# Moving the block sums of a fused attention and feed-forward kernel from GpSimd to VectorE, with earlier operand splits and loads

## The chip, the cores and the metric

The kernel runs on one core of one Trainium2 chip. The metric is the device time of one execution in microseconds: before the change 1176.31 us (median of 3 runs, 1173.57 to 1179.24). The engines of the core work side by side, each through its own queue in the order in which the program issued: TensorE (PE) multiplies matrices, VectorE (DVE) and ScalarE (ACT) work element by element, GpSimd (POOL) does too and also issues DMAs, and SyncE (SP) only issues DMAs. PSUM, where PE writes, is used here in 8 banks.

## What is computed

The inputs are q, k and v of 8 batches, 12 heads, 448 positions and 64 channels, and two weight matrices in float64, w_in (768 x 2048) and w_out (2048 x 768).

```
scores = scale * np.matmul(q, k.transpose(0, 1, 3, 2)) - np.log(S)
attn = 1.0 / (1.0 + np.exp(-scores))
x = attn @ v                      # laid out as 3584 tokens x 768
h = x @ w_in
g = 0.5 * h * (1.0 + erf(h / sqrt(2)))
out = g @ w_out
```

So it is an attention with a sigmoid in place of softmax, and behind it a GELU feed-forward layer over 3584 tokens.

## The kernel before

**Attention** comes first: 24 units (a batch and two pairs of heads each), whose results are written to DRAM (`scr_x`). PE is busy throughout. Beside it DVE and ACT *decode* the weights: a float64 arrives as two 32-bit words and is turned into a float32 with five DVE and two ACT instructions a chunk (class `Decoder`, L97 to L192). There are 40 chunks: 16 of w_in (768 wide, each written to `scr_f`) and 24 of w_out (512 wide). `dec.to(n)` sets at which places of the program the work up to chunk n is issued.

**The feed-forward layer** runs over 4 blocks of 896 tokens (two batches). Each product is made exact enough by splitting both operands in a high and a low half (ACT casts to `hi`, DVE computes `lo = src - hi`) and adding three matmuls, `hi*lo + lo*hi + hi*hi` (`terms`, L467). Block 0 computes its first product (x times w_in) plainly, `ffn1_plain`: 16 rows of w_in, 36 matmuls each. All other products use a Strassen-Winograd scheme: 2 x 2 blocks, seven products (p = 1 to 7) in place of eight, and sums of blocks as operands. `ffn1` (first product, blocks 1 to 3) runs 56 steps of 9 matmuls in the order `IN_ORDER`: the chains (1, 2), (6, 7, 4) and (5, 3). `ffn2` (second product, all blocks) runs 28 steps of 18 matmuls in the order `OUT_ORDER`: p = 1, 2, 5, 6, 3, 7, 4 with four column groups c each. So the feed-forward part is seven stages of 504 matmuls behind one of 576.

Who prepares what:

- **Weights** (class `Weights`, L197): SP loads a unit into `wst` (3 places), ACT casts it (L233) and DVE subtracts (L234) into `whl` (4 places). A unit serves one step of `ffn2` or two of `ffn1`. `prepare_to` runs 3 to 4 units ahead of PE, and `load_to` another 2 to 3.
- **Sums of weight blocks** (`mix`, L88): four sums on POOL, for 6 groups of w_out (`flush`, in `ffn1_plain`, as soon as four chunks are decoded) and for 8 groups of w_in (`remix`, in `ffn2` of block 0). POOL issues the DMAs that write the sums to `scr_out` and `scr_in`, whence SP loads units.
- **Operands of `ffn2`** (`build`, L609): ACT casts a tile of `g` (L262) and DVE subtracts (L263) into `op`, two steps before PE uses it. Before the first step `build(0)` and `build(1)` are issued together.
- **Sums of operands**: `difference_g` (L501, in the first product), L672, L674 and L675 (in `ffn2`, in place in the tiles of g) and `x_sum` (L553), all on POOL. `x_split` (L558) splits the x operands of the next block; `x_load` fetches their four tiles with 12 DMAs on SP's queue.
- **Results** leave PSUM through ACT (L648, L650, L655, L585) or a sum on DVE (L589, L591, L595, L652, L660, L664).

The order on every engine is that of the program text; nothing is moved by a scheduler.

## Time and profile before

| | us |
|---|---|
| median of 3 runs | 1176.31 (1173.57 to 1179.24) |
| profiled execution | 1176.96 |
| its span, first to last instruction | 1175.2 |
| PE busy | 1071.8 (91%) |
| DVE busy | 838.6 (71%) |
| ACT busy | 607.3 (52%) |
| POOL busy | 400.8 (34%) |
| mean granted PE clock | 0.961 |

Times in the profile count from the first instruction. The stages begin, by the first matmul of each, at 0 (attention), 256.1 (`ffn1_plain`), 385.9 (`ffn2` of block 0), 517.6 (`ffn1` of block 1), 628.8 (`ffn2`), 740.9 (`ffn1` of block 2), 844.8 (`ffn2`), 959.4 (`ffn1` of block 3) and 1063.3 (`ffn2`). A row such as `L234 DVE TENSOR_TENSOR whl<-wst,whl` names the line of the kernel, the engine, the operation, and the tile written and those read. In square brackets, or behind the last bar, stands the idle time of the engine before the instruction and what ended it. "PE busy" counts a matmul as long as it is in the pipeline, so a busy PE may still be slow; what counts is how soon each step of 18 matmuls follows the other.

### The profile page before, as it was taken

Reading aid. Unit: us, or ns where it says so; the run is one execution under the profiler, and the core shown is the slowest. Engines: PE = TensorE matmul, PEld = TensorE weight load, DVE = VectorE, ACT = ScalarE, POOL = GpSimd, SP = SyncE. Lnnn points to the kernel's source line nnn. Section 1 sums busy time; section 2 is a strip of 40 time slices with the busy share of each in tenths; the row PEclk is TensorE's granted clock in tenths of the full one; section 3 lists DMA queues with packets and bytes.
Section 4 is the critical chain, followed back from the end, with each engine's and each line's share of the span. In section 5 each row is a group of like instructions: output and inputs, shape, how many; then the busy total and the mean of one; then the engine's idle time right before and its main releaser. Section 6 shows DMA issues by size and latency. Waiting matters only on the chain. (4 is left out here: it accounts for less than half of the span.)

```text
span 1175.2 us, 15595 instructions
## 1 busy us (share of the span) xinstructions
PE 1071.8 (91%) x5930; PEld 924.2 (79%) x5930; DVE 838.6 (71%) x852; ACT 607.3 (52%) x810; POOL 400.8 (34%) x316
## 2 busy tenths in 40 slices
PE   9999999999986876789997979999798999998988
PEld 4455455559986876679997969999797899987988
DVE  4777777648895579985566799556659974665895
ACT  5887887764343533236354624544454354445532
POOL 0111111037878479972011482000219310011640
PEclk9999999999998888889999989999899899998999
DMA  9999998775764695574332625433353443332332
GB/s 283 305 307 300 306 294 271 218 240 183 251 211 142 217 347 180 205 249 157 118 108 85 221 67 168 145 108 108 94 189 104 130 155 114 116 96 92 118 108 98
DMA packets 96378, 211.80 MB, mean 180 GB/s; under 512 B 10288, under 2 KB 47536, under 8 KB 96304
## 3 DMA queue, kind: packets, MB, share of 16 engines
q1 hardware_dynamic: 84560, 171.24, 46.8%
q0 software_dynamic: 11584, 39.33, 8.8%
q8 instruction: 47, 0.77, 0.3%
q10 hardware_dynamic: 160, 0.23, 0.1%
q14 instruction: 27, 0.22, 0.1%
HBM read 160.43 MB, written 50.33 MB: 179 GB/s over the span
## 5 line engine op out<-in xcount | busy, mean ns | idle before, releaser
L472 PE MATMUL pf<-op,whl 128*128 128x448 f32 x2016 | 415.2, 369 | 76.8 <-DVE op L263 49.5
L472 PEld LDWEIGHTS pf<-op,whl 128*128 128x128 f32 x2016 | 398.0, 199 | 94.0 <-DVE op L263 57.8
L234 DVE TENSOR_TENSOR whl<-wst,whl 128x768 fp32r<-128x768 f32 x212 | 282.1, 1332 | 182.0 <-ACT whl L233 181.8
L233 ACT CAST whl<-wst 128x768 fp32r<-128x768 f32 x212 | 175.9, 830 | 278.8 <-PE pf L472 198.7
L472 PE MATMUL pf<-xh_p,whl 128*128 128x448 f32 x1008 | 277.7, 355 | 11.8 <-DVE tmp L595 7.3
L472 PEld LDWEIGHTS pf<-xh_p,whl 128*128 128x128 f32 x1008 | 192.1, 191 | 15.4 <-issue 6.3
L263 DVE TENSOR_TENSOR op<-g,op 128x896 fp32r<-128x896 f32 x112 | 184.5, 1651 | 4.7 <-ACT op L262 4.7
L472 PE MATMUL pf<-xl_p,whl 128*128 128x448 f32 x504 | 179.1, 355 | 4.0 <-DVE xl_p L263 4.0
L328 ACT ACTIVATE a<-sc 128x896 f32<-128x896 f32 x144 | 121.8, 920 | 53.4 <-PE sc L345 53.4
L501 POOL TENSOR_TENSOR g<-g,g 128x896 f32<-128x896 f32 x16 | 34.3, 2145 | 299.2 <-ACT g L498 299.2
L383 PE MATMUL pav<-a,v 128*64 128x448 f32 x576 | 119.1, 548 | 0.0
L472 PE MATMUL pf<-xh,whl 128*128 128x448 f32 x384 | 106.0, 357 | 4.5 <-DVE whl L234 3.5
L262 ACT CAST op<-g 128x896 fp32r<-128x896 f32 x112 | 104.2, 935 | 4.7 <-POOL g L672 2.4
L472 PEld LDWEIGHTS pf<-xl_p,whl 128*128 128x128 f32 x504 | 96.1, 191 | 4.6 <-DVE xl_p L263 4.4
L498 ACT ACTIVATE g<-tmp 128x448 f32<-128x448 f32 x72 | 42.6, 621 | 98.4 <-DVE tmp L595 98.4
L383 PEld LDWEIGHTS pav<-a,v 128*64 128x64 f32 x576 | 37.0, 136 | 68.0 <-issue 63.6
L412 POOL DMA_DIRECT2D scr_x<-x x24 | 17.3, 719 | 208.7 <-DVE x L409 208.7
L472 PEld LDWEIGHTS pf<-xh,whl 128*128 128x128 f32 x384 | 73.5, 191 | 6.2 <-DVE whl L234 4.2
L409 DVE COPY x<-pav 128x448 f32<-128x448 f32 x48 | 29.9, 624 | 63.7 <-PE pav L383 40.9
L472 PE MATMUL pf<-xl,whl 128*128 128x448 f32 x192 | 68.6, 357 | 0.5 <-DVE xl L263 0.5
L672 POOL TENSOR_TENSOR g<-g,g 128x896 f32<-128x896 f32 x16 | 34.1, 2137 | 97.1 <-DVE op L263 97.0
L129 ACT ACTIVATE me<-me 128x512 f32<-128x512 int32 (+1 forms) x40 | 29.1, 728 | 55.1 <-DVE me L118 55.1
(70 smaller groups left out, 1213.1 us busy)
## 6 DMA issues: line engine op xcount, KB each, us to landing
wst<-scr_out SPq DMA_DIRECT2D x112, 384.0 KB, 3.1
wst<-scr_in SPq DMA_DIRECT2D x84, 384.0 KB, 3.0
v<-v_dram SPq DMA_DIRECT2D x24, 512.0 KB, 5.5
raw<-w_in_dram SPq DMA_DIRECT2D x16, 768.0 KB, 8.3
raw<-w_out_dram SPq DMA_DIRECT2D x24, 512.0 KB, 5.5
scr_x<-x POOLq DMA_DIRECT2D x24, 448.0 KB, 6.8
...
```

The costliest lines, as they stand in the source:

```text
L129: nc.scalar.activation(e.bitcast(F32), e.bitcast(I32), AF.Relu, bias=1151.0 * 2**23, scale=-8.0)
L233: nc.scalar.copy(hl[:, 0], t)
L234: nc.vector.tensor_tensor(hl[:, 1], t, hl[:, 0], op=ALU.subtract)
L262: nc.scalar.copy(hi, src)
L263: nc.vector.tensor_tensor(lo, src, hi, op=ALU.subtract)
L328: nc.scalar.activation(to, sc, AF.Sigmoid, bias=NEG_LOG_S, scale=SCALE)
L383: nc.tensor.matmul(pav[rows(j)], vals[u][:, p, j, c], a[:, j], start=p == 0 and c == 0, stop=p == 1 and c == FULL - 1,)
L409: nc.vector.tensor_copy(xs[u][:, p], bank(u, p))
L472: nc.tensor.matmul(bank, a, braid(m), **flags)
L498: nc.scalar.activation(straight(dst), unbraid(src), AF.Gelu)
L501: nc.gpsimd.tensor_tensor(g[0, 1][c], g[0, 1][c], g[0, 0][c], op=sub)
L672: nc.gpsimd.tensor_tensor(t1, g22, t1, op=sub)
```

## The change

- All sums that POOL computed (`mix`, `difference_g`, `x_sum` and the three sums in `ffn2`) are issued on DVE. POOL keeps its DMAs alone. The sum for p = 4 (L675) moves from the steps of p = 6 to those of p = 3.
- `scr_out` has one tensor for both halves of a column group, so a group is written with 7 DMAs instead of 14.
- `build` becomes a function of its own. The first two operands of an `ffn2` are split ahead: in block 0 in the last two rows of `ffn1_plain`, in the other blocks at (5, 3) and (5, 7) of `ffn1`.
- In attention 24 chunks are decoded instead of 22: 16 at the rate of before, one a unit, and 8 in the last six units. There the `hi` cast of p = 0 goes from ACT to DVE. `ffn1_plain` decodes the other 16 over 13 rows.
- `x_load` is issued at step 0 of `ffn2` instead of step 6, the first two `x_sum`s at step 7 instead of step 16. `x_split` of 6, 7, 5 and 3 stands at other places of `ffn1`; the `hi` half of x operand 7 gets a place of its own (the tag `s`), a fourth beside the three of `raw`.
- The sums of w_in come in two stages: groups 0 to 3 at steps 2, 8, 14 and 20 of `ffn2` of block 0, where `recopy` also copies the unmixed parts of groups 4 to 7 from DRAM to DRAM; and groups 4 to 7 in the first steps of `ffn1` of block 1, in tiles of g that are not yet in use.

```diff
     def mix(a, s):
-        a11, a12, a21, a22 = (a[:, i] for i in range(4))
-        s1, s2, s3, s4 = (s[:, i] for i in range(4))
-        nc.gpsimd.tensor_tensor(s1, a21, a22, op=ALU.add)
...
+        a11, a12, a21, a22 = a
+        s1, s2, s3, s4 = s
+        nc.vector.tensor_tensor(s1, a21, a22, op=ALU.add)
...
                 for p in (1, 2, 5, 6, 3, 7, 4):
                     src = parts[p].rearrange("p (h f n) -> p h f n", h=2, f=2)
-                    for h in range(2):
-                        nc.gpsimd.dma_start(scr_out[p, 2 * c + h][:, :, e], src[:, h])
+                    nc.gpsimd.dma_start(scr_out[p, c][:, :, :, e], src)
...
-    AHEAD, BEGIN = 22, 2
+    AHEAD, BEGIN, LATE = 24, 2, 18
...
-            if p == 0 and u > 2:
+            if p == 0 and 2 < u <= LATE:
                 nc.scalar.copy(hi, raw)
             else:
                 nc.vector.tensor_copy(hi, raw)
...
-                dec.to(min((u + 0.5 - BEGIN) * AHEAD / (total - BEGIN), AHEAD))
+                work = u + 0.5 - BEGIN
+                if work > NF:
+                    work = NF + (work - NF) * (AHEAD - NF) / (total - LATE)
+                dec.to(min(work, AHEAD))
...
         def difference_g(g, c):
-            nc.gpsimd.tensor_tensor(g[0, 1][c], g[0, 1][c], g[0, 0][c], op=sub)
+            nc.vector.tensor_tensor(g[0, 1][c], g[0, 1][c], g[0, 0][c], op=sub)
...
-                dec.to(AHEAD + 1.5 * (f + 1))
+                dec.to(AHEAD + (len(CHUNKS) + 0.5 - AHEAD) * (f + 1) / (NF - 3))
+                if f >= NF - 2:
+                    build(0, g, f - NF + 2)
...
         def x_sum(tag, b, p, a, c):
             t = x_tile(tag, f"x{b}_p{p}") if tag else c
-            nc.gpsimd.tensor_tensor(
+            nc.vector.tensor_tensor(
...
         def x_split(ops, b, p):
-            hi = ring(f"xh{b}_p{p}")
+            hi = ring(f"xh{b}_p{p}", "s" if p == 7 else "raw")
...
-                if (p, j) == (1, 2):
-                    x_split(ops, b, 6)
-                after = {(1, KF - 1): 7, (2, KF - 1): 4, (6, KF - 1): 5, (7, KF - 1): 3}
+                if b == 1 and p == 1 and KF // 2 <= j + 3 < KF:
+                    remix(j + 3, g)
+                after = {(1, 4): 6, (1, 6): 7, (2, KF - 1): 4, (7, 2): 5, (6, KF - 1): 3}
                 if (p, j) in after:
                     x_split(ops, b, after[p, j])
+                if (p, j) == (5, 3):
+                    build(b, g, 0)
+                if (p, j) == (5, KF - 1):
+                    build(b, g, 1)
...
-            build(0)
-            build(1)
             for n, (p, c) in enumerate(OUT_ORDER):
                 hl = W.get()
-                build(n + 2)
+                build(b, g, n + 2)
...
                 if ahead[0] == 5:
                     t1, g22 = g[0, 1][ahead[1]], g[1, 1][ahead[1]]
-                    nc.gpsimd.tensor_tensor(t1, g22, t1, op=sub)
+                    nc.vector.tensor_tensor(t1, g22, t1, op=sub)
                 if p == 6:
-                    nc.gpsimd.tensor_tensor(g11, t2, g11, op=sub)
-                    nc.gpsimd.tensor_tensor(g21, g21, t2, op=sub)
-                if b == 0 and n % 3 == 2 and n // 3 < KF:
-                    remix(n // 3)
+                    nc.vector.tensor_tensor(g11, t2, g11, op=sub)
+                if p == 3:
+                    nc.vector.tensor_tensor(g21, g21, t2, op=sub)
+                if b == 0 and n % 6 == 2 and n // 6 < KF // 2:
+                    remix(n // 6)
+                    recopy(n // 6 + KF // 2)
                 if b + 1 < NB:
-                    if n == 6:
+                    if n == 0:
                         x = x_load(b + 1)
-                    if (p, c) == (3, 0):
+                    if (p, c) == (2, 3):
                         nxt[5] = x_sum("xt3", b + 1, 5, x[0, 1], x[0, 0])
...
```

Three places of the order show what is moved. The first is DVE around the steps of p = 5 in `ffn2` of block 2 (operands `op_8` to `op_11`; `g_01`, `g_11` and `g_00` are tiles of g, `x_01` and the like tiles of the next block's x). Before:

```order
L234 TENSOR_TENSOR whl_7387<-wst_7338,whl_7387 128x768
L263 TENSOR_TENSOR op_8_7392<-g_01_0_6408,op_8_7392 128x896
L234 TENSOR_TENSOR whl_7430<-wst_7364,whl_7430 128x768
L263 TENSOR_TENSOR op_9_7435<-g_01_1_6409,op_9_7435 128x896
L234 TENSOR_TENSOR whl_7466<-wst_7390,whl_7466 128x768
L263 TENSOR_TENSOR op_10_7471<-g_01_2_6410,op_10_7471 128x896
```

while POOL had in a row, at the same place of the program:

```order
L672 TENSOR_TENSOR g_01_2_6410<-g_11_2_6418,g_01_2_6410 128x896
L672 TENSOR_TENSOR g_01_3_6411<-g_11_3_6419,g_01_3_6411 128x896
L674 TENSOR_TENSOR g_00_0_6404<-g_01_0_6408,g_00_0_6404 128x896
L675 TENSOR_TENSOR g_10_0_6412<-g_10_0_6412,g_01_0_6408 128x896
L674 TENSOR_TENSOR g_00_1_6405<-g_01_1_6409,g_00_1_6405 128x896
```

DVE at this place in the changed kernel:

```order
L237 TENSOR_TENSOR whl_7339<-wst_7290,whl_7339 128x768
L266 TENSOR_TENSOR op_8_7344<-g_01_0_6344,op_8_7344 128x896
L682 TENSOR_TENSOR g_01_0_6344<-g_11_0_6352,g_01_0_6344 128x896
L237 TENSOR_TENSOR whl_7366<-wst_7316,whl_7366 128x768
L266 TENSOR_TENSOR op_9_7371<-g_01_1_6345,op_9_7371 128x896
L682 TENSOR_TENSOR g_01_1_6345<-g_11_1_6353,g_01_1_6345 128x896
L574 TENSOR_TENSOR x_p_7402<-x_01_7194,x_00_7190 128x1344
L574 TENSOR_TENSOR x_01_7194<-x_11_7198,x_01_7194 128x1344
L237 TENSOR_TENSOR whl_7405<-wst_7342,whl_7405 128x768
L266 TENSOR_TENSOR op_10_7410<-g_01_2_6346,op_10_7410 128x896
L682 TENSOR_TENSOR g_01_2_6346<-g_11_2_6354,g_01_2_6346 128x896
```

One sum more a step, and at step 7 two x sums, stand in DVE's queue ahead of the weight and operand splits that follow.

The second is ACT where `ffn1` of block 2 passes into `ffn2` (`op_0` and `op_1` are the first two operands). Before:

```order
L233 CAST whl_7186<-wst_7128 128x768
L498 ACTIVATE g_01_3_6411<-tmp_7200 128x448
L498 ACTIVATE g_01_3_6411<-tmp_7212 128x448
L262 CAST op_0_7219<-g_00_0_6404 128x896
L262 CAST op_1_7222<-g_00_1_6405 128x896
L233 CAST whl_7225<-wst_7158 128x768
```

In the changed kernel:

```order
L504 ACTIVATE g_11_3_6355<-tmp_7122 128x448
L265 CAST op_1_7125<-g_00_1_6341 128x896
L236 CAST whl_7128<-wst_7067 128x768
L504 ACTIVATE g_01_3_6347<-tmp_7142 128x448
L504 ACTIVATE g_01_3_6347<-tmp_7154 128x448
L236 CAST whl_7161<-wst_7097 128x768
L265 CAST op_2_7166<-g_00_2_6342 128x896
```

The cast of `op_1` now stands ahead of the last two GELUs of the first product, and that of `op_0` thirteen rows further up.

The third is SP around the x loads of the same stage. Before:

```order
L223 DMA wst_7364<-scr_out_2_106 128x768
L223 DMA wst_7390<-scr_out_3_107 128x768
L259 DMA x_00_7414<-scr_x 128x2x224 x3
L259 DMA x_01_7418<-scr_x 128x2x224 x3
L259 DMA x_11_7422<-scr_x 128x2x224 x3
L259 DMA x_10_7426<-scr_x 128x2x224 x3
L223 DMA wst_7433<-scr_out_0_108 128x768
```

In the changed kernel:

```order
L226 DMA wst_7131<-scr_out_0_98 128x768
L226 DMA wst_7164<-scr_out_0_98 128x768
L262 DMA x_00_7190<-scr_x 128x2x224 x3
L262 DMA x_01_7194<-scr_x 128x2x224 x3
L262 DMA x_11_7198<-scr_x 128x2x224 x3
L262 DMA x_10_7202<-scr_x 128x2x224 x3
L226 DMA wst_7209<-scr_out_1_99 128x768
```

The twelve loads now come ahead of the weights of the third step of p = 2, that is six units earlier in SP's queue.

More of the change, by code (lines that the diff above doesn't have):

```diff
@@ L78, in tile_sigmoid_attention_gelu_ffn @@
     scr_out = {
-        pc: tc.dram_tile([P, 2, KE, P], F32, name=f"scr_out{pc[0]}_{pc[1]}") for pc in OUT_ORDER
+        (p, c): tc.dram_tile([P, 2, 2, KE, P], F32, name=f"scr_out{p}_{c}")
+        for p in range(1, 8)
+        for c in range(2)
     }
@@ L160, in flush @@
                 (c, e), a = self.pending.pop(0)
[L161 to L162 removed]
+                s = self.pool.tile([P, 4 * QUAD], F32, tag="s", name=f"s{c}_{e}", bufs=1)
+                quads = [t[:, i * QUAD : i * QUAD + QUAD] for t in (a, s) for i in range(4)]
+                parts = mix(quads[:4], quads[4:])
                 for p in (1, 2, 5, 6, 3, 7, 4):
                     src = parts[p].rearrange("p (h f n) -> p h f n", h=2, f=2)
[L165 to L166 removed]
+                    nc.gpsimd.dma_start(scr_out[p, c][:, :, :, e], src)
                 self.groups += 1
@@ L265, in ring @@
     def ring(name, tag="raw"):
-        n, bufs = {"raw": (RAW, 3), "me": (2 * WU, 2), "wd": (4 * QUAD, 2)}[tag]
-        return sb.tile([P, n], F32R, tag=tag, name=name, bufs=bufs)
+        n, bufs = {"raw": (RAW, 3), "me": (2 * WU, 2), "wd": (4 * QUAD, 2), "s": (4 * QUAD, 1)}[tag]
+        return (late if tag == "s" else sb).tile([P, n], F32R, tag=tag, name=name, bufs=bufs)
     def braid(m):
@@ L500, in difference_g, with build @@
         def difference_g(g, c):
-            nc.gpsimd.tensor_tensor(g[0, 1][c], g[0, 1][c], g[0, 0][c], op=sub)
+            nc.vector.tensor_tensor(g[0, 1][c], g[0, 1][c], g[0, 0][c], op=sub)
+        source = {1: (0, 0), 2: (1, 0), 5: (0, 1), 6: (0, 1), 3: (1, 1), 7: (0, 0), 4: (1, 0)}
+        built = {}
+        def build(b, g, n):
+            if n >= len(OUT_ORDER):
+                return
+            p, c = OUT_ORDER[n]
+            src = g[source[p]][c].rearrange("p f s -> p (f s)")
+            op = ring(f"op{b}_{n}")[:, : 4 * S]
+            op = op.rearrange("p (h n) -> p h n", h=2)
+            split(op[:, 0], op[:, 1], src)
+            built[n] = op
         def ffn1_plain(g):
@@ L693, in ffn2, with remix, recopy @@
             return nxt
-        def remix(j):
-            a = sb.tile([P, 4 * QUAD], F32, tag="wd", name=f"a{j}", bufs=2)[:, : 2 * WU]
+        def remix(j, g=None):
+            if g:
+                c = 2 * (j % 2)
+                tiles = [g[0, 1][c], g[1, 1][c], g[0, 1][c + 1], g[1, 1][c + 1]]
+                tiles = [t.rearrange("p f s -> p (f s)")[:, :WU] for t in tiles]
+            else:
+                a = sb.tile([P, 4 * QUAD], F32, tag="wd", name=f"a{j}", bufs=2)
+                t = ff.tile([P, 4 * QUAD], F32, tag="s", name=f"sin{j}", bufs=1)
+                tiles = [x[:, i * WU : i * WU + WU] for x in (a, t) for i in range(2)]
             for i in range(2):
-                nc.sync.dma_start(a[:, i * WU : (i + 1) * WU], scr_f[i * KF + j])
-            s = ff.tile([P, 4, QUAD], F32, tag="s", name=f"sin{j}", bufs=1)[:, :, :OP]
-            parts = mix(a.rearrange("p (q n) -> p q n", q=4), s)
+                nc.sync.dma_start(tiles[i], scr_f[i * KF + j])
+            quads = [t[:, i * OP : i * OP + OP] for t in tiles for i in range(2)]
+            parts = mix(quads[:4], quads[4:])
             for p, part in parts.items():
+                if not (g and p in (1, 2, 4)):
+                    n = IN_ORDER.index((p, j))
+                    nc.gpsimd.dma_start(scr_in[n // 2][:, n % 2], part)
+        def recopy(j):
+            for p, f, half in ((1, j, 0), (2, j, 1), (4, j + KF, 1)):
                 n = IN_ORDER.index((p, j))
-                nc.gpsimd.dma_start(scr_in[n // 2][:, n % 2], part)
+                src = scr_f[f][:, half * OP : half * OP + OP]
+                nc.gpsimd.dma_start(scr_in[n // 2][:, n % 2], src)
         g = slots(0)
```

22 lines of the change are left out of this document (5 added, 17 removed).

## The prediction

> **What bounds the kernel now.** I read the table of stages first, then the waits of PE, then the timeline of DVE and POOL where PE waits. Its columns are the length of a stage, the busy time and count of each engine, the granted PE clock and the DMA share.
>
> ```profile
> core 0: us, PE busy (x) PEld busy (x) DVE busy (x) ACT busy (x) POOL busy (x), PEclk, DMA share, GB/s
> 0.00:256.10 256.10, 253.26 (x1827) 129.18 (x1827) 174.03 (x236) 197.97 (x242) 28.83 (x43) 1.00 0.89 279
> 256.10:385.90 129.80, 111.91 (x576) 109.74 (x576) 96.62 (x112) 52.90 (x89) 104.45 (x112) 0.94 0.65 211
> 385.90:517.60 131.70, 105.84 (x504) 101.42 (x505) 108.86 (x68) 51.14 (x65) 103.12 (x94) 0.87 0.69 239
> 517.60:628.80 111.20, 99.56 (x506) 97.20 (x505) 69.16 (x80) 51.38 (x76) 23.18 (x17) 0.97 0.41 131
> 628.80:740.90 112.10, 102.33 (x504) 98.43 (x505) 94.26 (x71) 52.44 (x66) 47.04 (x17) 0.95 0.43 138
> 740.90:844.80 103.90, 96.29 (x507) 94.88 (x505) 60.30 (x76) 50.73 (x75) 7.10 (x4) 1.00 0.37 117
> 844.80:959.40 114.60, 104.85 (x504) 100.46 (x505) 94.07 (x71) 52.43 (x66) 47.03 (x17) 0.93 0.42 135
> 959.40:1063.30 103.90, 96.30 (x507) 94.88 (x505) 60.31 (x76) 50.70 (x75) 7.11 (x4) 1.00 0.37 117
> 1063.30:1175.20 111.90, 101.51 (x504) 98.06 (x504) 81.01 (x68) 47.62 (x61) 32.94 (x13) 0.95 0.32 103
> ```
>
> Attention keeps PE busy. The seven stages of 504 matmuls do the same work in 104 to 132 us: the more POOL computes, the longer they are and the lower the granted clock. How fast a step can be shows where PE never waits. Two weight casts of ACT follow each other as PE frees a place, and DVE beside them is undisturbed although POOL is generating DMAs:
>
> ```profile
> 406.43 0.83 ACT L233 CAST whl<-wst 128x768 fp32r<-128x768 f32 x1 [1.30 <-PE pf L472]
> 409.84 0.83 ACT L233 CAST whl<-wst 128x768 fp32r<-128x768 f32 x1 [1.73 <-PE pf L472]
> 407.30 0.96 DVE L234 TENSOR_TENSOR whl<-wst,whl 128x768 fp32r<-128x768 f32 x1
> 408.17 1.08 DVE L263 TENSOR_TENSOR op<-g,op 128x896 fp32r<-128x896 f32 x1
> 408.36 1.61 POOL L703 DMA_DIRECT2D scr_in<-sin x3
> ```
>
> A step of 18 matmuls takes 409.84 - 406.43 = 3.41 us, so a stage of 28 steps cannot be under 95.5 us, nor the plain one of 32 under 109.1. DVE needs 0.87 us for the weight (start to start) and 1.0 for the operand, far less than a step. Now the place where PE does wait:
>
> ```profile
> PE pf L472 <- DVE op L263: 49.5, 24, 12.8
> PE pf L472 <- ACT op L262: 25.2, 5, 13.9
> ...
> 890.86 2.86 DVE L234 TENSOR_TENSOR whl<-wst,whl 128x768 fp32r<-128x768 f32 x1
> 893.64 2.97 DVE L263 TENSOR_TENSOR op<-g,op 128x896 fp32r<-128x896 f32 x1
> ...
> 892.85 2.81 POOL L674 TENSOR_TENSOR g<-g,g 128x896 f32<-128x896 f32 x1
> 895.63 2.92 POOL L675 TENSOR_TENSOR g<-g,g 128x896 f32<-128x896 f32 x1
> ...
> 457.42 14.27 DVE L234 TENSOR_TENSOR whl<-wst,whl 128x768 fp32r<-128x768 f32 x1
> ...
> 458.66 2.10 POOL L674 TENSOR_TENSOR g<-g,g 128x896 f32<-128x896 f32 x1
> 468.81 2.06 POOL L675 TENSOR_TENSOR g<-g,g 128x896 f32<-128x896 f32 x1
> ```
>
> While POOL adds, the same DVE instructions take 2.9 us, each as long as POOL's; weight and operand then need 5.7 us a step against PE's 3.41. Once a weight split hung for 14.27 us, from just before POOL's run of sums at 458.66 until that run was over. So PE waits for operands, not because DVE has too much work but because DVE and POOL exclude each other when both read two tiles. This bounds the `ffn2` stages, and the granted clock (0.87 to 0.95 there, 1.00 where POOL is quiet) falls with the waits.
>
> **The change part by part.** I build the span anew from the floors and add what stays.
>
> *The sums leave POOL.* Afterwards POOL issues only DMAs, and the rows at 407 to 410 show DVE undisturbed by these. Of the excess over 95.5 us, the four `ffn2` stages (36.2, 16.6, 19.1 and 16.4 us) lose nearly all. DVE receives the sums. Its prices, with three widths that no POOL sum touched:
>
> ```profile
> L263 DVE TENSOR_TENSOR xl<-xl,xh 128x1344 fp32r<-128x1344 f32 x4 | 6.1, 1555 | 6.8 <-ACT xh L262 6.8
> L595 DVE TENSOR_TENSOR tmp<-pf,g 128x448 f32<-128x448 f32 x72 | 42.4, 616 | 10.3 <-PE pf L472 10.3
> ```
>
> A sum over 896 is the shape of the operand split, 1.0 us; over 1344 it is 1.5. A `mix` sum over 512 or 384 is not in the trace on DVE: from 768 to 896 the time grows by 0.12 us in 128 columns, which gives an estimate of 0.71 and 0.59 us; the bounds are 0.4 (proportional to width) and 0.96 (the 768-wide one). I take the estimates. In an `ffn2` DVE then has 28 weights x 0.87 + 26 operands x 1.0 + 12 sums x 1.0 + 4 x sums and 2 x splits x 1.5 + 15 evictions x 0.6 = 24.4 + 26 + 12 + 9 + 9 = 80 us of 95.5; block 0 adds 16 `mix` sums x 0.59 = 9, so 89. It fits, and the queue decides: an operand is asked for two steps (6.8 us) ahead and is ready some 2.8 us after its turn (ACT 0.83 + 0.93, DVE 1.0), so DVE may fall 4 us behind before PE notices. Step 7 holds 1.9 of splits, one sum and two x sums, 5.9 us, 2.5 over; step 9 is back in time. I put 0.5 to 1.5 us on each `ffn2`.
>
> *`mix` in DVE's queue.* DVE now waits where POOL did: for the loads of w_in's two rows, and for the last group's DMAs to leave the scratch tile. Behind a waiting `mix` stand weight splits, which ACT and PE wait for. In `ffn2` of block 0 two of the four groups have their loads issued behind a result store, so DVE reaches `mix` some 3 us early and blocks; with its 2.4 us that is beyond the 4 us by 1 to 2 us, twice. In `ffn1` of block 1 four groups follow in 13.6 us, at some 3 us of slack in the weights: 2.5 us, between 0 and 8. Together I take 4 + 2.5 of 0 to 18.
>
> *Operands ahead.* Where `ffn1` ends, PE stands 3.6 us until the first two operands are cast, then 2.3 us for the DVE half; three stages have this. The rows are those of the `ffn1` of block 2 with the first matmuls behind it, and the piece of the chain of waits at 1063.
>
> ```profile
> L472 PE MATMUL pf<-xh_p,whl 128*128 128x448 f32 x336 | 91.9, 353 | 4.0 <-DVE tmp L595 2.4 <-DVE g L589 1.5
> L472 PE MATMUL pf<-op,whl 128*128 128x448 f32 x3 | 1.0, 387 | 3.6 <-ACT op L262 3.6
> 1063.27 2.26 DVE op L263
> ```
>
> Built ahead it is gone: the last split is asked for 3.4 us before the stage ends and needs 2.8. What stays of an `ffn1` (103.9 - 95.5 - 3.6 = 4.8 us) are chiefly the waits of the first row above, at the heads and tails of the chains where an eviction stands behind an x split on DVE. The change moves these splits and adds `difference_g` (1.0 us) at the last tail: I take 5.5 a stage, of 2 to 8.
>
> *The plain stage.* The largest single wait is its end:
>
> ```profile
> 371.24 1.90 POOL L91 TENSOR_TENSOR s<-wd 128x512 f32<-128x512 f32 x1 [2.83 <-DVE wd L143]
> 382.61 0.83 ACT L233 CAST whl<-wst 128x768 fp32r<-128x768 f32 x1 [11.31 <-DMA wst<-scr_out]
> 384.93 2.62 ACT L262 CAST op<-g 128x896 fp32r<-128x896 f32 x3
> ...
> 364.16 0.68 DVE L138 SCALAR_TENSOR_TENSOR me<-raw,me 128x512 uint32<-128x512 uint32 x1
> 366.55 0.69 DVE L122 SCALAR_TENSOR_TENSOR me<-raw,me 128x512 uint32<-128x512 uint32 x1
> ```
>
> The last chunk is decoded at 371.2, its group summed and written, and ACT waits for that unit with the first operands queued behind it: 14 us. Five decode instructions take 3.1 us (364.16 to 367.24). DVE's work in the changed stage is 16.5 chunks x 3.1 + 16 weights x 0.87 + 24 sums x 0.71 + 6 others x 1.0 to 1.5 = 51 + 14 + 17 + 7 = 89 of 109 us, so DVE keeps up with PE; chunk 39, issued after row 12 (256 + 13 x 6.82 = 345), ends near 352, and the unmixed part that the first waiting unit needs is written before the sums. That leaves about 10 us for write, load and cast until PE is through at 365; I take 3 us of wait for the stage, of 0 to 14.
>
> *The rest.* In attention DVE gets two chunks (6.2 us) and six casts (0.6 us) more over the last six units; DVE was busy 174 of 256 us, so I cost it at nothing (3 us if an operand is late). The x loads:
>
> ```profile
> 651.82 6.51 SPq L259 DMA_DIRECT2D x<-scr_x x12
> 664.40 0.83 ACT L233 CAST whl<-wst 128x768 fp32r<-128x768 f32 x1 [2.49 <-DMA wst<-scr_out]
> ```
>
> They held SP for 6.5 us and made ACT wait 2.5 for the next weight; with weights three units ahead PE felt neither, and I leave it so at step 0.
>
> *The sum.* Floors: 256.1 + 109.1 + 7 x 95.5 = 1033.7. What stays: plain 3; `ffn2` of block 0 4; the `ffn1`s 8, 5.5 and 5.5; the other `ffn2`s 1.5, 1.5 and 0.5, and 3.5 for the last sum and store behind PE. That is 33, so a span of 1066.7; the profiled execution of before was 1177.0 for a span of 1175.2, so 1.8 more: **1068 us**. That execution is 0.7 above the median, within the spread of the runs.
>
> **The rivals.** *DVE becomes the bound.* It has 80 to 89 of 95.5 us in `ffn2`, and its order is fixed: if each of 56 splits loses 0.3 us to its ACT partner, a stage becomes 97 to 106, and with its waits the kernel gains 20 to 45 us less, some 1100. For it: the blocks at `mix`. Against it: before the first sums (386 to 420) the pair of splits ran without a PE wait.
>
> *The sums were not the partner.* If DMA generation on POOL holds DVE too, the waits stay where POOL issues, in the first two stages, and half to all of what they are above their floors (129.8 - 109.1 + 36.2 = 57 us) stays: 1096 to 1125. The row at 408.36 speaks against it.
>
> *DVE waits for its own writes (slower).* One scratch tile serves all groups of w_out, and DVE's next `mix` needs the seven DMAs of the last to have landed:
>
> ```profile
> L166 POOL DMA_DIRECT2D scr_out<-s x48 | 37.3, 1484 | 1.1 <-DMA scr_out<-wd 1.0
> scr_out<-s POOLq DMA_DIRECT2D x48, 128.0 KB, 5.9
> ```
>
> An issue of half the size took 1.5 us on POOL, so a doubled one takes 1.5 to 3.0, a group 7 x 3.0 + 5.9 = 27 us at worst; groups come every 4 chunks, 3.15 rows, 21.5 us. At worst the stage grows by 6 x 5 = 30 us. To end behind 1177 each of six groups would have to take 21.5 + 109 / 6 = 40 us, an issue 4.8 us. By the Trainium skill (SBUF — State Buffer, "SBUF: two separate sides") VectorE's two-port operations keep GpSimd from writing descriptors until they end; were that to hold for all that DVE now does, this rival would be near. Its section "Who interferes with whom" allows a two-input sum beside a GpSimd instruction that does not read, and the row at 408.36 agrees, with 0.54 us an issue beside two such splits; the decode's operations are not tested by that row.
>
> **How the numbers follow.** The forecast 77%, DVE as the bound 13%, the wrong partner 5%, the wait for writes 5%, of which I count all as slower though only its far end is. About 0.5% (6 us) is what a measurement here can tell from no change. Faster then has 93%, the same 2%, slower 5%. The forecast's own range follows from the bounds above: all waits at their low ends give 1050, the high ends of the plain stage, of `mix` and of the `ffn1`s together 1068 + 11 + 11 + 8 = 1098. To 1105 it also takes in most of the first rival.
>
> **What would show it.** Right: no two-input DVE instruction of 768 or 896 columns over 1.2 us; a clock of 1.00 in blocks 1 to 3; `ffn2` stages at 95 to 100 us and `ffn1` at 99 to 103; no operand wait at the passage from `ffn1`. Wrong: PE still waiting on L266 with DVE above 95% busy (first rival), long splits beside POOL's DMAs (second), DVE idle before L93 on `scr_out` DMAs (third). The plain stage's passage is the weakest step: should ACT still wait there for `scr_out`, up to 11 us come back.

## The result: 1099 us, and the stages afterwards

The changed kernel takes 1099.24 us (median of 4 runs, 1097.34 to 1101.73), the kernel before, on the same chip, 1177.48 (1173.57 to 1179.24): a ratio of 0.9341, 95% interval 0.9310 to 0.9372. It is 78 us faster. 109 were forecast, so the time lies inside the range of 1050 to 1105 and 31 us above the number.

First the view by stages of the changed kernel, with the columns as for the kernel before (length, busy time and count of PE, PEld, DVE, ACT and POOL, the granted PE clock, the DMA share and GB/s). The stages are attention, plain, and then `ffn2` and `ffn1` by turns.

```profile
0.00:259.70 259.70, 256.33 (x1827) 131.08 (x1827) 181.67 (x251) 196.04 (x241) 28.82 (x43) 1.00 0.89 279
259.70:377.40 117.70, 111.77 (x576) 110.07 (x577) 83.18 (x130) 49.37 (x82) 31.08 (x43) 0.97 0.73 237
377.40:482.70 105.30, 98.49 (x507) 96.54 (x505) 88.05 (x102) 53.04 (x67) 21.32 (x40) 0.97 0.75 248
482.70:593.90 111.20, 98.78 (x505) 95.86 (x505) 68.19 (x93) 49.88 (x73) 8.54 (x16) 0.98 0.50 163
593.90:694.30 100.40, 97.60 (x506) 96.30 (x505) 82.98 (x90) 52.89 (x68) 0.00 (x0) 0.98 0.52 158
694.30:799.20 104.90, 98.15 (x506) 95.97 (x505) 62.00 (x78) 50.62 (x73) 0.00 (x0) 0.98 0.38 112
799.20:896.90 97.70, 95.97 (x507) 95.00 (x506) 81.58 (x89) 52.60 (x67) 0.00 (x0) 1.00 0.54 163
896.90:1000.30 103.40, 96.63 (x505) 94.73 (x504) 60.55 (x77) 50.29 (x73) 0.00 (x0) 1.00 0.37 114
1000.30:1100.00 99.70, 95.80 (x505) 94.84 (x504) 73.92 (x83) 48.23 (x63) 0.00 (x0) 1.00 0.41 119
```

The four `ffn2` stages, 131.7, 112.1, 114.6 and 111.9 us before, are 105.3, 100.4, 97.7 and 99.7: 67 of the 75 us between the two spans. The plain stage gave 12.1. The three `ffn1` stages gave 0.0, -1.0 and 0.5, although the wait where they end is gone; attention lost 3.6. Against the floors of the prediction the excess is 3.6, 8.6, 9.8, 15.7, 4.9, 9.4, 2.2, 7.9 and 4.2 us, 66 in place of 33 (in the profiled execution, which took 1101.73 us, 2.5 above the median).

Now the waits of PE (total in us, times, longest), and the groups of the operations that the prediction priced (busy us, mean ns of one, idle time before them):

```profile
PE pf L478 <- DVE tmp L616: 16.0, 12, 3.2
PE pf L478 <- DVE op L266: 6.8, 4, 4.9
...
PE pf L478 <- ACT xh L265: 5.0, 1, 5.0
PE pf L478 <- ACT y L658: 4.3, 2, 2.7
...
L237 DVE TENSOR_TENSOR whl<-wst,whl 128x768 fp32r<-128x768 f32 x212 | 202.1, 954 | 133.6 <-ACT whl L236 133.5
L266 DVE TENSOR_TENSOR op<-g,op 128x896 fp32r<-128x896 f32 x112 | 121.2, 1084 | 9.1 <-ACT op L265 9.1
L168 POOL DMA_DIRECT2D scr_out<-s x24 | 17.3, 753 | 57.0 <-DVE s L93 52.5 <-DVE s L96 1.9 <-PE pf L478 1.7
L93 DVE TENSOR_TENSOR s<-wd 128x512 f32<-128x512 f32 x6 | 4.1, 691 | 0.2
L93 DVE TENSOR_TENSOR sin<-a 128x384 f32<-128x384 f32 x4 | 2.2, 560 | 8.5 <-DMA a<-scr_f 8.5
L93 DVE TENSOR_TENSOR g<-g 128x384 f32<-128x384 f32 x4 | 2.2, 558 | 11.5 <-DMA g<-scr_f 11.5
```

No split of a weight or of an operand takes over 1.15 us any more; before, beside POOL's sums, they took 2.9 us, some 3.9, and three in block 0 6.8, 9.2 and 14.27. The wait for operands, 49.5 us before, is 6.8. The largest wait is now for the sums of `ffn1`'s evictions (L616), and `mix` waits 8.5 and 11.5 us for its loads.

### The profile page after: what moved, and what is told of

Read it like the earlier page. It is cut to its first block, busy times and chain, and to the rows that moved or that the text cites. A ratio compares the mean times of both kernels' runs of the same rounds, so it can differ in the third digit from the quotient of the medians.

```text
span 1100.0 us, 15452 instructions
## 1 busy us (share of the span) xinstructions
PE 1049.5 (95%) x5930; PEld 910.4 (83%) x5930; DVE 782.1 (71%) x989; ACT 603.0 (55%) x805; POOL 89.8 (8%) x142
## 4 chain that ended last, share of the span: by engine, by line
PE 75%; DVE 8%; DMA 7%; ACT 5%; issue 4%; SPq 1%; DVEq 0%; ACTq 0%
PE pf L478 53%; PE pav L386 9%; PE sc L348 8%; DVE whl L237 2%; PE sc_t L365 2%; ACT whl L236 2%; DVE tmp L616 2%; DMA wst<-scr_out 2%; PE pav L399 2%; DMA g<-scr_f 1%; DMA xl<-scr_x 1%; ACT g L504 1%; DMA wst<-scr_in 1%; DMA a<-scr_f 1%; DMA x<-scr_x 1%
## 5 line engine op out<-in xcount | busy, mean ns | idle before, releaser
L478 PE MATMUL pf<-op,whl 128*128 128x448 f32 x2016 | 388.2, 355 | 11.5 <-DVE op L266 6.8
L478 PEld LDWEIGHTS pf<-op,whl 128*128 128x128 f32 x2016 | 382.8, 190 | 16.3 <-DVE op L266 8.2
L237 DVE TENSOR_TENSOR whl<-wst,whl 128x768 fp32r<-128x768 f32 x212 | 202.1, 954 | 133.6 <-ACT whl L236 133.5
L266 DVE TENSOR_TENSOR op<-g,op 128x896 fp32r<-128x896 f32 x112 | 121.2, 1084 | 9.1 <-ACT op L265 9.1
L348 PE MATMUL sc<-lo,hi 64*128 64x448 f32 x282 | 56.9, 393 | 1.0 <-ACT a L331 1.0
L348 PEld LDWEIGHTS sc<-lo,hi 64*128 64x128 f32 x282 | 26.9, 186 | 36.7 <-ACT me L134 14.8
L323 DVE TENSOR_TENSOR lo<-qk,hi 128x896 fp32r<-128x896 f32 x47 | 51.2, 1089 | 1.5 <-ACT hi L320 0.4
```

The source lines that it names most:

```text
L237: nc.vector.tensor_tensor(hl[:, 1], t, hl[:, 0], op=ALU.subtract)
L266: nc.vector.tensor_tensor(lo, src, hi, op=ALU.subtract)
L323: nc.vector.tensor_tensor(lo, raw, hi, op=ALU.subtract)
L348: nc.tensor.matmul(sc[:, j], ks[rows(j), 1, keys], braid(qs[rows(j), 0]) if braided else qs[rows(j), 0], start=n == 0, stop=n == last,)
L478: nc.tensor.matmul(bank, a, braid(m), **flags)
```

## The experiments

The theory: POOL's sums and DVE's two-input instructions exclude each other, so the engine of the sums is what counts; what stayed above the floors are late steps in DVE's and SP's queues. The rivals: the gain came from the new places of the work; or DVE has too much in its queue. All ratios are to the kernel before, run beside it on the same chip. The stage lengths below come from one execution of each kernel, and one stage of the same code differs between them: the attention of the changed kernel took 257.6 to 260.0 us in the nine kernels that have it. So differences of a stage below some 2 us say little by themselves.

| kernel | median, us | ratio, 95% interval |
|---|---|---|
| the change | 1099.24 | 0.9341 (0.9310 to 0.9372) |
| pool_sums | 1163.20 | 0.9893 (0.9863 to 0.9922) |
| before_dve_sums | 1134.57 | 0.9652 (0.9625 to 0.9679) |
| one_stage | 1113.84 | 0.9457 (0.9425 to 0.9489) |
| pool_kinds (leaves out sums) | 1157.31, one run | |
| late_diff | 1096.69 | 0.9326 (0.9303 to 0.9349) |
| pool_diff | 1093.80 | 0.9287 (0.9254 to 0.9320) |
| remix_two | 1089.15 | 0.9247 (0.9215 to 0.9278) |
| flush_late | 1091.82 | 0.9276 (0.9248 to 0.9303) |
| x_spread | 1094.23 | 0.9292 (0.9265 to 0.9318) |
| attn_22 | 1100.84 | 0.9352 (0.9327 to 0.9378) |
| all_four | 1061.22 | 0.9016 (0.8989 to 0.9043) |
| all_four_22 | 1063.55 | 0.9036 (0.9014 to 0.9058) |

### The engine of the sums, alone and with the rest

*All sums back on POOL, the rest of the change kept:*

```diff
-        nc.vector.tensor_tensor(s1, a21, a22, op=ALU.add)
+        nc.gpsimd.tensor_tensor(s1, a21, a22, op=ALU.add)
```

(and likewise the other sums of `mix`, `difference_g`, `x_sum` and the three sums of `ffn2`).

> The changed kernel with all its block sums put back on POOL (those of the decoded pieces, of the ffn2 blocks, of x and of the group differences); operands built ahead, the fourth place for x, 24 chunks in attention and w_in in two stages stay. Theory (DVE and POOL exclude each other, so the sums' engine is the cause): DVE's two-input instructions of 768 and 896 columns are again 2 to 3 us beside POOL's sums, the weight groups' mean (954 ns in the changed kernel) goes back above 1.2 us, the ffn2 stages stand at 108 to 118 us, and at least half of the 78 us gained is lost: 1140 to 1175. Rival (the gain came from operands built ahead and from the new places of the work): the stages stay within 5 us of those of the changed kernel, 1095 to 1120.

*The kernel before, with its sums on DVE in the same places* (the same edit the other way round):

> The kernel before, with its POOL sums issued on VectorE in the same places and nothing else changed. Theory: the ffn2 stages of blocks 1 to 3 fall from 112 to 115 us to 97 to 103; the passages from ffn1 to ffn2 (5.9 us each in three stages) and the 14 us at the end of the plain stage stay; 1110 to 1135. Rival (without operands ahead, DVE's longer queue gives the time back): within 15 us of before, 1160 to 1190.

Both totals came out by the theory; of the `ffn2` stages that it named, two lie above its ranges (129.2 us in block 0 of `pool_sums`, 103.6 in block 3 of `before_dve_sums`). The mean weight split went back to 1.27 us in the first and is 0.96 in the second. Rows of the views by stages: of `pool_sums` the first two `ffn2` stages and the `ffn1` of block 2; then of `before_dve_sums` the same two `ffn2` stages.

```profile
384.90:514.10 129.20, 106.82 (x505) 101.70 (x506) 104.73 (x72) 53.30 (x68) 86.00 (x72) 0.90 0.63 209
622.90:737.10 114.20, 101.56 (x505) 96.86 (x504) 96.92 (x73) 52.90 (x68) 49.59 (x18) 0.97 0.45 139
737.10:836.60 99.50, 96.31 (x506) 94.93 (x505) 58.63 (x74) 50.02 (x73) 5.83 (x3) 1.00 0.38 118
```

```profile
371.50:505.90 134.40, 111.07 (x505) 104.69 (x506) 96.09 (x119) 51.86 (x65) 32.51 (x60) 0.87 0.73 255
613.80:715.30 101.50, 99.54 (x505) 97.34 (x506) 81.53 (x88) 52.49 (x66) 0.00 (x0) 0.96 0.47 153
```

With the sums on POOL the `ffn2` of block 1 takes 114.2 us (112.1 in the kernel before); with the sums on DVE, and nothing else changed, 101.5. The sums alone give 40 us, all the rest alone 12, the two together 78. By the ratios the whole is some 24 us more than its parts, and one stage shows 26 of such an excess, the `ffn2` of block 0: 131.7 before, 129.2 in the one, 134.4 in the other, 105.3 with both. The other stages have smaller ones, up to 6 us and of both signs. One part of the expectation for `before_dve_sums` missed, and it concerns a step of the prediction: the 14 us at the end of the plain stage did not stay. That stage took 116.1 us, and the first operands followed it with a wait of 2.2. Putting `mix` on DVE was enough; the new pace of the decode was not needed for it.

*The sums of w_in in one stage.* This asks which of the other edits makes the `ffn2` of block 0 short.

```diff
-                if b == 0 and n % 6 == 2 and n // 6 < KF // 2:
-                    remix(n // 6)
-                    recopy(n // 6 + KF // 2)
+                if b == 0 and n % 3 == 2 and n // 3 < KF:
+                    remix(n // 3)
```

(and no `recopy`, and no `remix` in `ffn1` of block 1).

> The changed kernel with the sums of w_in all in ffn2 of block 0, a group every three steps, as before the change; sums still on VectorE. Theory (in the kernel before with its sums on VectorE this stage took 134.3 us against 105.3 here because eight groups of four sums and their loads stand in DVE's queue in one stage): ffn2 of block 0 rises to 120 to 130 us, ffn1 of block 1 falls from 111.2 to 103 to 105; 1106 to 1120. Rival (the 29 us came from the x sums issued earlier, the fourth place and the operands ahead): ffn2 of block 0 stays below 112, and the total is at most 1099.

The stage rose to 126.5 us and `ffn1` of block 1 fell from 111.2 to 104.8, 14.6 us in the total. So two stages for w_in bring 21.2 us in the first stage and give 6.4 back in the second, and only where DVE does the sums: with them on POOL the first stage stood at 129.2 with the two stages in place. PE waited 24.0 us for operands in the stage of `one_stage`, in ten places, with DVE busy 95.8 of its 126.5 us; `mix` on DVE waited 24.9 us for its loads there. It is the blocks in DVE's queue, not its work.

### What of POOL's work excludes DVE

The kernel before, with the three POOL sums of `ffn2` replaced in two blocks, so that these sums are left out there.

```diff
+            if b == 1:
+                nc.gpsimd.memset(t, 0.0)
+            elif b == 2:
+                nc.gpsimd.tensor_copy(t, x if x is not t else y)
+            else:
+                nc.gpsimd.tensor_tensor(t, x, y, op=sub)
```

> The kernel before, with the three POOL sums of ffn2 in another form in each block: a memset of the same 896 columns in block 1 (POOL reads nothing), a one-input copy in block 2, the two-input subtraction as it was in blocks 0 and 3. The sums of blocks 1 and 2 are thereby left out of the result. Theory 1 (the engines exclude each other only where POOL too reads two tiles): the ffn2 stages of blocks 1 and 2 both fall to 97 to 104 us, with no weight split over 1.2 us beside POOL's instructions; block 3 stays at 112. Theory 2 (any work of POOL on a tile excludes DVE): blocks 1 and 2 stay at 108 to 115. Theory 3 (one read is enough): block 1 falls, block 2 stays.

DVE and POOL in the timeline, first beside memsets, then beside copies, then beside sums (start, duration; a row of POOL stands for a run of x9, x8 and x5):

```profile
671.41 1.08 DVE L263 TENSOR_TENSOR op<-g,op 128x896 fp32r<-128x896 f32 x1
672.98 0.96 DVE L234 TENSOR_TENSOR whl<-wst,whl 128x768 fp32r<-128x768 f32 x1 [0.48 <-ACT whl L233]
669.71 7.15 POOL L607 MEMSET g<- 128x896 f32 x9 [3.65 <-DVE op L263]
...
880.92 1.81 DVE L263 TENSOR_TENSOR op<-g,op 128x896 fp32r<-128x896 f32 x1
882.65 1.68 DVE L234 TENSOR_TENSOR whl<-wst,whl 128x768 fp32r<-128x768 f32 x1
875.04 11.83 POOL L609 COPY g<-g 128x896 f32<-128x896 f32 x8 [3.43 <-DVE op L263]
...
1084.65 2.98 DVE L263 TENSOR_TENSOR op<-g,op 128x896 fp32r<-128x896 f32 x1
1087.55 2.85 DVE L234 TENSOR_TENSOR whl<-wst,whl 128x768 fp32r<-128x768 f32 x1
1083.93 14.09 POOL L611 TENSOR_TENSOR g<-g,g 128x896 f32<-128x896 f32 x5 [1.89 <-DVE op L263]
```

Beside memsets DVE keeps its 0.96 and 1.08 us. Beside copies the two engines take turns, 1.68 and 1.81; beside sums 2.85 and 2.98. So one tile read by POOL is enough, and writing alone does nothing: the third theory by the instructions. The rule in the Trainium skill (SBUF — State Buffer, "Who interferes with whom"), that a VectorE instruction with two SBUF inputs contends with a GpSimd instruction that reads SBUF but not with one that only writes, agrees with these rows. The stages do not follow the third theory: block 1 took 102.2 us and block 2, which should have stayed, 104.9 (112.1 and 114.6 before; block 3, unchanged, 111.2). A copy lengthens a split by less than a sum does (0.7 us against 1.9): weight and operand then need 3.5 us a step, about PE's 3.41.

### The waits that stayed

*`ffn1`.* The timeline of DVE, and of PE, at the end of the `ffn1` of block 2 in the changed kernel:

```profile
794.27 1.09 DVE L507 TENSOR_TENSOR g<-g,g 128x896 f32<-128x896 f32 x1 [0.67 <-ACT g L504]
795.28 0.62 DVE L616 TENSOR_TENSOR tmp<-pf,g 128x448 f32<-128x448 f32 x1
...
795.96 0.74 PE L478 MATMUL pf<-xh_p,whl 128*128 128x448 f32 x1 [3.23 <-DVE tmp L616]
```

The difference waits 0.67 us for ACT's GELU and takes 1.0, and behind it stands the eviction for which PE waits 3.23. Two cures were tried. *Later on DVE*, where j = 7 is the last step of the stage:

```diff
-                    if p == 3 and r == 1:
+                    if p == 3 and r == 1 and j < KF // 2:
                         difference_g(g, c)
+                    if (p, j) == (3, KF - 1):
+                        difference_g(g, c - 1)
+                        difference_g(g, c)
```

> The changed kernel, with the group differences of the last two groups issued behind the last eviction of the ffn1 chain instead of before it. Theory (the difference, waiting for ACT's GELU at the head of DVE's queue, holds back the eviction on which the last matmuls of ffn1 wait): the wait of PE at the tail of each of the three ffn1 stages falls from 3.6 to 1 us, as it was in the kernel before, 7 to 8 us in all: 1090 to 1094. Rival (the tail waits for the length of the add, GELU and x split themselves): the wait stays, 1097 to 1101.

*On POOL:*

```diff
-            nc.vector.tensor_tensor(g[0, 1][c], g[0, 1][c], g[0, 0][c], op=sub)
+            nc.gpsimd.tensor_tensor(g[0, 1][c], g[0, 1][c], g[0, 0][c], op=sub)
```

> The changed kernel with the group differences alone (twelve tiles over the three ffn1 stages and four in the plain stage) put back on POOL; every other sum stays on VectorE. Theory (in ffn1 the difference costs by standing in DVE's queue, where it waits for ACT's GELU and holds back the evictions behind it; on POOL it waits by itself and lengthens a split or two to 1.7 us, which have slack): the ffn1 stages of blocks 2 and 3 fall from 104.9 and 103.4 us to the 99.5 that they had with all sums on POOL, block 1 by some 5, together 10 to 14 us: 1085 to 1090. Rival (the exclusion of POOL and DVE costs as much as the queue): 1095 to 1102.

Later on DVE, the three `ffn1` stages fell by 2.3, 3.3 and 1.7 us, as the theory has it (the last step at the tail follows 1.8 us after the one before, 3.6 in the changed kernel). But the total fell by 2.5 us only, 0.9326 against 0.9341, which the intervals do not tell apart, and 1096.69 misses the 1090 to 1094 of the theory: the `ffn2` of block 2 was 4.3 us longer, with a wait of 3.0 for ACT that the changed kernel has there with 1.6, and a clock of 0.97 in place of 1.00. On POOL the stages of blocks 2 and 3 fell to 99.5, exactly as in `pool_sums`, and block 1 to 106.8, though again part of it went in `ffn2` (101.2 in place of 97.7 in block 2): 1093.80, a miss of the 1085 to 1090, and the lower of the two medians, though their intervals overlap. So it is the stages that speak for POOL, not the totals: this sum, which waits for another engine, did better in `ffn1` in a queue in which nothing stands behind it.

*Loads of the w_in groups two steps ahead of their sums.* SP, DVE and PE of the changed kernel in the `ffn2` of block 0:

```profile
450.62 1.46 SPq L635 DMA_DIRECT2D out_dram<-tmp  x3
452.72 0.91 SPq L717 DMA_DIRECT2D a<-scr_f  x2
...
458.24 0.56 DVE L93 TENSOR_TENSOR sin<-a 128x384 f32<-128x384 f32 x1 [3.72 <-DMA a<-scr_f]
...
463.73 1.49 PE L478 MATMUL pf<-op,whl 128*128 128x448 f32 x3 [4.94 <-DVE op L266]
```

The load stands behind three result stores and a weight load, DVE blocks 3.72 us at its `mix`, and PE then waits 4.94. In `ffn1` of block 1 DVE blocks four times in the same way (the 11.5 us above).

```diff
+                if b == 0 and n % 6 == 0 and n // 6 < KF // 2:
+                    remix_load(n // 6)
...
+                if b == 1 and p == 1 and KF // 2 <= j + 1 < KF:
+                    remix(j + 1, g)
                 if b == 1 and p == 1 and KF // 2 <= j + 3 < KF:
-                    remix(j + 3, g)
+                    remix_load(j + 3, g)
```

> The changed kernel with the loads of a w_in group issued two steps before its sums, in both stages, and nothing else moved. Theory (DVE stands at the first sum waiting for a load that was issued just ahead of it behind a result store, so that the next weights or operands are late): the 5.3 us wait in ffn2 of block 0 and the 4.1 and 3.6 us in ffn1 of block 1 go, with the slower clock behind them; ffn2 of block 0 at 98 to 101 us, ffn1 of block 1 at 104 to 107; 1087 to 1093. Rival (DVE has too much in its queue there, not a late load): the stages stay within 2 us, 1096 to 1101.

Measured 1089.15, as forecast. The two stages:

```profile
375.80:473.90 98.10, 96.39 (x505) 94.60 (x504) 87.83 (x102) 52.84 (x67) 21.36 (x40) 1.00 0.80 264
473.90:580.50 106.60, 98.12 (x506) 95.64 (x505) 69.50 (x95) 50.54 (x73) 8.57 (x16) 0.99 0.52 170
```

With 87.8 us of DVE work in 98.1 and a clock of 1.00, DVE is not the bound even in its fullest stage.

*The first w_out group one row later.* The start of the plain stage in the changed kernel (SP, POOL, ACT, PE), and then in `flush_late` (SP, ACT):

```profile
260.85 6.15 SPq L262 DMA_DIRECT2D xl<-scr_x  x6
260.56 1.50 POOL L168 DMA_DIRECT2D scr_out<-wd  x2
273.73 1.31 ACT L265 CAST xh<-xl 128x1344 fp32r<-128x1344 f32 x1 [6.42 <-DMA xl<-scr_x]
...
275.09 0.74 PE L478 MATMUL pf<-xh,whl 128*128 128x448 f32 x1 [4.96 <-ACT xh L265]
```

```profile
260.85 4.62 SPq L262 DMA_DIRECT2D xl<-scr_x  x6
267.80 1.31 ACT L265 CAST xh<-xl 128x1344 fp32r<-128x1344 f32 x1 [0.49 <-DMA xl<-scr_x]
```

```diff
-                if f == 0:
-                    dec.pool = ff
-                    dec.flush()
                 if f == 1:
                     for hi, lo in x1:
                         split(hi, lo, lo.bitcast(F32))
+                    dec.pool = ff
+                    dec.flush()
```

(and for this group the DMAs of the sums ahead of those of the unmixed parts).

> The changed kernel with the first group of w_out summed and written one row later in the plain stage, behind the split of the first x operands, its sums' DMAs ahead of those of its unmixed parts. Theory (POOL's first seven DMAs start beside the x loads and delay them, 6.15 us for six in place of 3.84, so that ACT's first cast of x is late): the 5.3 and 1.6 us waits near 275 us go or shrink below 2 together, and the plain stage falls from 117.7 to 110 to 113 us; 1092 to 1095. Rival (the x loads are late by themselves, being issued only when the last unit of attention is stored): the wait stays and the total with it, 1096 to 1102.

Measured 1091.82; the plain stage took 110.4 us, 1.3 over its floor, with the passage to `ffn2` without a wait. That the x loads are late by themselves is refuted. The edit moves the DMAs and reorders them, and the two were not tried apart. Nor is it known how much the doubled size of these DMAs does: in `before_dve_sums`, where POOL's first DMAs also leave at once but are half as large, PE waited 1.4 us for the x operand in place of 5.0.

*The x loads, three a step.* SP and ACT at the start of the `ffn2` of block 1 in the changed kernel:

```profile
595.95 6.23 SPq L262 DMA_DIRECT2D x<-scr_x  x12
...
608.24 0.83 ACT L236 CAST whl<-wst 128x768 fp32r<-128x768 f32 x1 [5.57 <-DMA wst<-scr_out]
```

```diff
-                    if n == 0:
-                        x = x_load(b + 1)
+                    if n < 4:
+                        x_load(b + 1, x, n)
```

> The changed kernel with the twelve x loads of an ffn2 issued three at a time over its first four steps instead of twelve at the first. Theory (they hold SP's queue for 6.2 us, so the next weight unit is loaded late, ACT waits 5.6 us for it and the operand casts and results behind it on ACT are late): no wait of PE on ACT's results over 0.5 us in ffn2 of blocks 1 and 2, these stages at 96 to 98 us (100.4 and 97.6 in the changed kernel), 1094 to 1097. Rival (the wait comes from ACT's own work at the start of the stage): waits of 2 to 3 us stay there, 1097 to 1102.

1094.23 us, and the two stages took 96.0 and 96.6 us, without a wait for ACT: by the theory. But the 100.4 us of block 1 overstates what the loads cost. The six other kernels that issue all twelve at step 0 as the change does (`late_diff`, `pool_diff`, `one_stage`, `remix_two`, `flush_late`, `attn_22`) took 96.9 to 102.0 us in these stages, four of them at most 97.8 in both, with waits for ACT of 0 to 3.0 us. Nor are the intervals of the two ratios quite apart. That spreading the loads removes this wait is shown; its price, between some 1 and 5 us a stage, is not settled.

*Two chunks fewer in attention.* `AHEAD` back to 22, and the casts of the last units back on ACT.

```diff
-    AHEAD, BEGIN, LATE = 24, 2, 18
+    AHEAD, BEGIN, LATE = 22, 2, 18
...
-            if p == 0 and 2 < u <= LATE:
+            if p == 0 and u > 2:
```

> The changed kernel with 22 chunks decoded in attention instead of 24, at one a unit to the end, and the casts of the last units back on ACT, as before the change. Theory (two more chunks and six casts on VectorE in the last six units make the units late, and the plain stage has room on VectorE for two chunks more): attention falls from 259.7 to 256 us, the plain stage stays within 1 us of 117.7: 1094 to 1097. Rival (the plain stage needs the lead: with two chunks more the weights or the passage to ffn2 are late): the plain stage and its passage grow by 3 us or more, 1099 to 1106.

A miss of both: attention fell by 4.3 us to 255.4, the plain stage stayed within 1 (118.6), and the total was the same, 1100.84. The gain was given back by a third way, in the `ffn2` of block 0, which rose from 105.3 to 110.6: PE waited 3.1 us there for ACT's results, which the changed kernel does not do in this stage, and PE's clock was 0.95 to 0.96 in the three stages behind attention. The x loads of the stage on SP, first in the changed kernel, then in `attn_22`, and ACT in `attn_22`:

```profile
373.51 7.87 SPq L262 DMA_DIRECT2D x<-scr_x  x12
...
373.73 9.22 SPq L262 DMA_DIRECT2D x<-scr_x  x12
...
389.04 0.83 ACT L236 CAST whl<-wst 128x768 fp32r<-128x768 f32 x1 [6.09 <-DMA wst<-scr_out]
```

The twelve x loads hold SP for 9.2 us in place of 7.9, and ACT waits 6.1 for a weight unit behind them, for which it does not wait in the changed kernel. The length of the loads cannot be all of it: in `pool_diff` they held SP for 9.3 us in this stage, and it took 107.3. What else in the later decode makes the weights late was not tried.

### All cures together

The four cures, with the group differences on POOL except the last of each stage, which stays on DVE behind the last eviction.

> The changed kernel with four repairs together: the first w_out group one row later, loads of the w_in groups two steps ahead, the x loads spread over four steps, and the group differences of ffn1 on POOL except the last of a stage, which stays on VectorE behind the last eviction. Theory (the waits that stayed are separate late steps, so their cures add): 7.3 from the first, 7.1 and 4.6 from the second, 3 from the third and 3.5 to 5.4 in each of three stages from the fourth, with the clock at full speed: some 35 us below the changed kernel, 1062 to 1070. Rival (a cure makes the next instruction in the queue late): 1072 to 1082.

Three stages of its view by stages, the `ffn2` of block 0 and of block 1 and the `ffn1` of block 2:

```profile
368.20:467.20 99.00, 96.45 (x506) 94.68 (x505) 87.77 (x102) 52.92 (x67) 21.33 (x40) 1.00 0.80 272
...
568.60:664.50 95.90, 95.76 (x505) 94.91 (x505) 83.63 (x90) 53.02 (x68) 0.45 (x1) 1.00 0.54 166
664.50:764.00 99.50, 96.32 (x506) 94.94 (x505) 58.66 (x74) 49.97 (x73) 5.85 (x3) 1.00 0.39 118
```

1061.22 us, 38 below the changed kernel (0.9016 against 0.9341), 0.8 under the range of the theory. The cures more than add: one by one they gave 10.1 (`remix_two`), 7.4 (`flush_late`), 5.0 (`x_spread`) and 5.4 us (`pool_diff`), 28 in all. The clock is 1.00 in every stage, which no single cure reached; what else the other 10 us are made of was not separated. The `ffn2` of block 1 takes 95.9 us, 0.4 over the floor that the prediction set.

> The same four repairs, and 22 chunks decoded in attention as before the change. Theory: 3 to 4 us below the kernel with the four repairs, 1058 to 1067. Rival (the plain stage, now without its wait at the start, needs the two chunks' lead): the same or up to 5 us above it.

1063.55 us; the intervals of the two ratios overlap (0.9014 to 0.9058 and 0.8989 to 0.9043), so the two chunks are worth nothing measurable here either way. The rival has the number and not the reason: the plain stage took 110.3 us in both, so it did not need the lead. Attention was 1.4 us shorter, the `ffn2` of block 0 4.2 longer, with PE waiting 5.3 us for operands in place of 1.7.

## Why the prediction was right, and where its sum was short

The direction and the cause were right; that the time lies in the range is in part luck. 1099 us is above 1098, the high end of the forecast's own bounds, and inside only by the part of the range that was added for the rival that DVE becomes the bound. It is even that rival's number (some 1100), but not by its mechanism, as shown below. At the other end, the low ends of the waits, added to the floors, give 1047 and not 1050 (1033.7 + 6 for the `ffn1`s, 2 for the `ffn2`s, 3.5 at the end and 1.8). Of the signs named ahead, two held: no split over 1.2 us, and no operand wait where `ffn1` passes into `ffn2`. The others held in part or not: the clock was 1.00 in three of six stages, two of the four `ffn2` stages were at most 100 us, and no `ffn1` was at most 103.

**The sums leave POOL: right.** The floor of 3.41 us a step was reached once the rest was cured (95.9 us), the splits went back to 0.95 and 1.08 us, and the two kernels that move only the sums, in either direction, show that this is the cause: 40 us with nothing else changed. The prices of the moved sums were right too: 691 ns at 512 columns and 560 at 384, estimated at 710 and 590.

**The rivals.** DVE as the bound is refuted by `all_four`: 87.8 us of DVE work fit in 99.0. In the changed kernel DVE was busy 88.1 of the 105.3 us of its fullest stage, and it stood idle for loads and for ACT in front of the waits of PE. That DMA issues and not sums were the partner is refuted by `before_dve_sums`, where POOL issues as many DMAs as before. That DVE waits for its own writes did not come: `mix` of w_out waited 0.2 us in six groups, and an issue took 0.75 us, under the 1.5 to 3.0 that I had bounded it by. In `all_four` it did come, with 2.6 us.

**What stayed above the floors: undersized, 66 us in place of 33.** The missing 33.3 us are 3.6 in attention, 5.6 in the plain stage, 5.8 in the `ffn2` of block 0, 7.7, 3.9 and 2.4 in the `ffn1`s, and 3.4, 0.7 and 0.2 in the other `ffn2`s. By their steps:

- *`ffn1`, "I take 5.5 a stage, of 2 to 8".* This is the worst step. I had named the difference at the last tail with its 1.0 us, but not what stands behind it, nor that it waits for ACT first: 3.2 us of PE at the tail, three times (1.5 in `late_diff`), and 9.4 and 7.9 us a stage; on POOL the same stages are 4.0 over the floor. The queue that an operation joins has to be followed instruction by instruction, as I did for `mix` and not for this one.
- *`mix` in DVE's queue, "4 + 2.5 of 0 to 18".* The mechanism was as described, its size not: one block of 3.72 us made PE wait 4.94 in `ffn2`, and in `ffn1` of block 1 the four blocks of 11.5 us in all made a stage 6.3 us longer than the next `ffn1`. Loads issued earlier take 7.2 and 4.6 us off the two stages.
- *The plain stage, "I take 3 us of wait".* The passage that I called the weakest step cost nothing. The wait came at the other end: with POOL free, its first DMAs leave at once and delay the x loads. I had looked for this collision at the end of the stage alone. A thing that becomes faster starts its transfers earlier, and here that cost 7.3 us.
- *The x loads, "PE felt neither, and I leave it so at step 0".* At step 0 PE did feel them: 2 waits for ACT, 4.3 us in this execution, gone with the loads spread out. In other kernels with the same loads the wait was between 0 and 3.0 us a stage.
- *Attention, "I cost it at nothing (3 us if an operand is late)".* The bound of 3 was the right size: 3.6 here, and 257.6 to 260.0 us in the nine kernels with this attention against 255.4 to 256.5 in the five without the two chunks and the casts (`before` and `attn_22` among them).

**The clock** was predicted at 1.00 in blocks 1 to 3 and was 0.98 in three of these six stages. The view by windows, in four short windows behind waits of PE: of 4.94 us, of 3.22 and 3.23 us (the tails of two `ffn1` stages), and of 2.67 us (for ACT, in the `ffn2` of block 1):

```profile
463.70:467.20 3.50, 3.47 (x9) 3.18 (x10) 3.50 (x4) 0.00 (x0) 1.16 (x3) 0.50 0.98 290
592.10:595.60 3.50, 3.46 (x18) 3.46 (x19) 2.01 (x3) 2.17 (x3) 0.00 (x0) 1.00 0.00 0
796.00:799.20 3.20, 3.20 (x9) 2.92 (x10) 1.80 (x2) 2.10 (x3) 0.00 (x0) 0.54 0.00 0
...
610.40:613.90 3.50, 3.50 (x12) 3.24 (x13) 2.59 (x3) 2.38 (x4) 0.00 (x0) 0.62 0.43 117
```

At 3.41 us for 18 matmuls, the 9 in the first window lost 1.8 us and the 9 in the third 1.5; my sum counted waits at their own length. Of the three tail waits (3.22, 3.23 and 3.22 us) only the second had this. The Trainium skill (TensorE: Matmul & The Clock Gate, "What's actually happening") has the clock at half rate after an idle window of about 3.4 us, and says that this window runs freely. These rows agree in the half rate (0.50 and 0.54) and in that more counts than the length of a wait; they do not agree in the length, since waits of 3.23 and 2.67 us, shorter than that window, were followed by a slower clock.
